# One written order from the end of attention on: expert 0 spread over five units, routing in thirds, seven-product outputs from the first chunk

## The chip, the cores and the metric

The kernel runs on one core of a Trainium2 chip. The core has five engines with a queue each: TensorE (PE in the profile, with its weight loads shown as PEld), VectorE (DVE), ScalarE (ACT), GpSimd (POOL) and SyncE (SP). The metric is the device time of one execution in microseconds; the median of three runs is quoted. Lower is better.

## The reference

Two parts follow each other. The first is attention over 4 batches, 8 heads, 768 tokens of 64 elements, in 8 blocks of 96 tokens; a small matrix per head, normalised five times, mixes the blocks of keys and values. The second is a mixture of 8 experts over all 3,072 tokens, and every expert works on every token:

```
x = attn_out.transpose(0, 2, 1, 3).reshape(3072, 512)
P = exp(x @ w_gate - max)
for _ in range(8):
    P /= P.sum(1, keepdims=True) + 1e-9
    P /= P.sum(0, keepdims=True) + 1e-9
    P *= N / E
for e in range(8):
    h = maximum(x @ w1[e], 0)          # 512 -> 1024
    out += P[:, e:e+1] * (h @ w2[e])   # 1024 -> 512
```

The eight rounds that normalise P need the logits of all tokens, so they can't start before attention has ended, and no expert's output can be weighted before they are done.

## The kernel before

**Attention and expert 0.** Attention goes batch by batch. While a batch of attention is computed, expert 0 is applied to the batch before it, by the plain formula, unweighted; its outputs are kept in `osbl` (24 tiles of 128 tokens) and are scaled by P later (`scale0`, two tiles at a time on ACT). So when attention ends, expert 0 is still to be done for the last batch: two runs of 384 tokens, each with eight hidden steps (four 384-column products and a relu, L299 and L301) and three output tiles of eight 512-column products in two halves (L306), with a copy (L314).

**Experts 1 to 7.** The tokens are cut into three chunks of 1,024 per expert, 21 chunks in all. The product of two 2 x 2 block matrices is formed with seven block products instead of eight. For the hidden layer, `hidden` does it for one of the four column groups of a chunk; this is called a unit. Its steps `p1` to `p7` are two 512-column products each (L508), with copies and relus on ACT and relu sums on DVE (L497) in between. It needs sums of weight blocks (`sum_w`, on GpSimd) and of token blocks (`sum_x`, three parts `p` of the tokens, four operations each on DVE, L454, one of which overwrites a part of the token matrix `xtT`). A unit with `fork` copies its first product into a second PSUM bank and accumulates on both; a unit without it keeps a copy in SBUF and adds it on DVE.

For the outputs, `Pair` does the same with two tiles of 128 tokens: steps `q1` to `q7`, four 256-column products each (L631). It needs sums of hidden blocks (`sums`, three operations on GpSimd, L621), a difference `s3` (`rest`), and sums of second-layer weights (`sum_w2`, eight operations on GpSimd, L444). `plain` is the ordinary form of an output tile: eight 512-column products (L597). Results are weighted by P and added to `osbl` on DVE (`gather`, L581).

**The order.** `pin` keeps an instruction in program order on its engine; what isn't pinned is placed by a scheduler, which moves instructions of one engine past one another. From the end of attention to L695 the work is in three generators: expert 0's last batch (`tail0`), the routing (`balance`, eight rounds of five DVE operations, a product with a matrix of ones that sums over the partitions, and three more DVE operations) and `sum_x`. They run beside the four units of the first chunk, which are without `fork` and, like the routing, not pinned:

```
works, n = [first_units(), tail0], 0
while works:
    works = [w for w in works if next(w, 0) is None]
    n += 1
    if n % 3 == 0:
        next(chain, 0)
        next(xs, 0)
```

Then comes the main loop over `r` (L722), all of it pinned. Turn `r` does unit `r % 4` of chunk `1 + r // 4`, step by step in turn with output steps: those of the first chunk in the plain form for `r` up to 4 (`flat`), and from `r = 5` on those of pair `r - 5` and the rest of the pair before it. `weights(n)` issues n operations of GpSimd's queue of weight sums. At its end the last two pairs of the last chunk are done in the plain form.

**PSUM.** Eight banks: five in a ring for hidden products, three in a ring (`oacc`) for outputs.

Of the kernel before, what the change touches and what calls it, by code (L numbers as in the profile page):

```python
# [25 lines left out]
def kernel(  # L26
# [394 lines left out]
    def ring(name, n):  # L421
        tiles = [ps.tile([128, 512], F32, name=f"{name}{j}") for j in range(n)]
        at = [0]

        def take():
            at[0] += 1
            return tiles[(at[0] - 1) % n]
        return take

# [6 lines left out]
    def sum_w2(e):  # L436
        w2s[e] = (wcp.tile([128, 4, 4, Dm // 2], BF16, name="w2e") if e % 2 else
                  w2q.tile([128, 4, 4, Dm // 2], BF16, name="w2s"))
        for k in (0, 2):
            b11, b12 = (w2t[e][:, k:k + 2, d:d + 256] for d in (0, 256))  # L440
            b21, b22 = (w2t[e][:, 4 + k:6 + k, d:d + 256] for d in (0, 256))
            t1, t2, t3, t4 = (w2s[e][:, j, k:k + 2, :] for j in range(4))
            for a, b, c in ((b12, b11, t1), (b22, t1, t2), (b22, b12, t3), (b21, t2, t4)):
                pin(nc.gpsimd.tensor_tensor(out=c, in0=a, in1=b, op=ALU.subtract))  # L444
                yield
# [3 lines left out]
    def sum_x(p):  # L449
        ta, tb = (slice(1024 * p + 512 * i, 1024 * p + 512 * i + 512) for i in range(2))  # L450
        b11, b12, b21, b22 = (xtT[:, k:k + 2, t] for k in (0, 2) for t in (ta, tb))
        x1, x2, x4 = (xc[:, j, :, 512 * p:512 * p + 512] for j in range(3))
        for a, b, c in ((b12, b11, x1), (b22, x1, x2), (b22, b12, b12), (b21, x2, x4)):
            pin(nc.vector.tensor_tensor(out=c, in0=a, in1=b, op=ALU.subtract))  # L454
            yield

    def balance(bank):
        onesc = mpc.tile([128, 128], F32)
        nc.vector.memset(onesc, 1.0)
        I128 = mpc.tile([128, 128], F32)  # L460
        nc.vector.tensor_copy(I128, Ibig)
        gm = mpc.tile([128, 1], F32)
        nc.vector.reduce_max(out=gm, in_=glog.rearrange("p t e -> p (t e)"), axis=AX.X)
        gmps = bank()[:, 0:128]
        nc.tensor.matmul(gmps[0:1, :], gm, I128, start=True, stop=True)
        gm1 = mpc.tile([1, 1], F32)
        nc.vector.reduce_max(out=gm1, in_=gmps[0:1, :], axis=AX.X, negate=True)
        yield
        gnps = bank()[:, 0:128]
        nc.tensor.matmul(gnps[:, 0:1], onesc[0:1, :], gm1, start=True, stop=True)  # L470
        gneg = mpc.tile([128, 1], F32)
        nc.vector.tensor_copy(gneg, gnps[:, 0:1])
        nc.scalar.activation(out=glog, in_=glog, func=AF.Exp, bias=gneg)

        rs2 = mpc.tile([128, NT], F32)
        cs2 = mpc.tile([128, E], F32)
        cs1 = mpc.tile([128, E], F32)
        yield
        for it in range(8):
            nc.vector.reduce_sum(out=rs2, in_=glog, axis=AX.X)  # L480
            nc.vector.tensor_scalar_add(rs2, rs2, 1e-9)
            nc.vector.reciprocal(out=rs2, in_=rs2)
            nc.vector.tensor_mul(glog, glog, mkap(rs2, [rs2.ap[0], rs2.ap[1], [0, E]]))
            nc.vector.reduce_sum(out=cs2, in_=glog.rearrange("p t e -> p e t"), axis=AX.X)  # L484
            csps = bank()[:, 0:128]
            nc.tensor.matmul(csps[:, 0:E], onesc, cs2, start=True, stop=True)
            nc.vector.tensor_scalar(out=cs1, in0=csps[:, 0:E], scalar1=float(E) / N,
                                    scalar2=1e-9 * E / N, op0=ALU.mult, op1=ALU.add)
            nc.vector.reciprocal(out=cs1, in_=cs1)
            nc.vector.tensor_mul(glog, glog, mkap(cs1, [cs1.ap[0], [0, NT], cs1.ap[1]]))  # L490
            yield
# [7 lines left out]
    def hidden(e, p, i, hT, s3, fork, hold, bank):  # L499
# [6 lines left out]
        def add(ps, wa, xa, first):  # L506
            for kk in range(2):
                hold(nc.tensor.matmul(ps, wa[:, kk, :], xa[:, kk, :],  # L508
                                      start=(first and kk == 0), stop=(kk == 1),
                                      skip_group_check=True))  # L510
# [14 lines left out]
        def p1():  # L525
            t["u"] = bank()
            add(t["u"], a11, b11, True)
            if fork:
                t["w"] = bank()
                hold(nc.scalar.copy(t["w"], t["u"]))  # L530
            else:
                t["p1"] = wide("p5")
                hold(nc.scalar.copy(t["p1"], t["u"]))

        def p2():
            if fork:
                add(t["w"], a12, b21, False)
                hold(relu(c11, t["w"]))
            else:
                w = bank()  # L540
                add(w, a12, b21, True)
                hold(relu_sum(c11, w, t["p1"]))

        def p6():
            add(t["u"], s2, x2, False)
            t["u2"] = wide("u2")
            hold(nc.scalar.copy(t["u2"], t["u"]))  # L547

        def p5():
# [3 lines left out]
            hold(nc.scalar.copy(t["p5"], t["v"]))  # L553

        def p7():
            add(t["u"], s3w, x3, False)
            hold(relu_sum(c22, t["u"], t["p5"]))

        def p3():
            add(t["v"], s4, b22, False)  # L560
            hold(relu_sum(c12, t["v"], t["u2"]))

        def p4():
            add(t["u"], a22, x4, False)
            hold(relu(c21, t["u"]))

        def rest():
            if s3 is None:
                pass
            elif fork:  # L570
                hold(nc.vector.scalar_tensor_tensor(out=s3[:, i, :], in0=t["w"], scalar=0.0,  # L571
                                                    in1=c12, op0=ALU.max, op1=ALU.subtract))
            else:
                hold(nc.vector.tensor_tensor(out=s3[:, i, :], in0=c11, in1=c12,
                                             op=ALU.subtract))

        return ([p1, p5, p6, p2, p7, p3, p4] if fork else [p1, p2, p6, p5, p7, p3, p4]), rest
# [92 lines left out]
    free = lambda ins: ins  # L670
    with banks("bk", 5) as bk, banks("op", 3) as op:
        bank = lambda: bk.tile([128, 512], F32, name="bk")
        tail0 = expert0(B - 1, lambda: hTb[1], bank,
                        lambda: op.tile([128, Dm], F32, name="oacc"))
        chain, xs = balance(bank), sum_x(0)
        for step in "TTCXTTTXCXXTTCTTTC":
            next({"T": tail0, "C": chain, "X": xs}[step])
        xs = sum_x(1)

        def first_units():  # L680
            for i in range(4):
                for f in hidden(1, 0, i, hTb[0], None, False, free, bank)[0]:
                    f()
                    yield

        works, n = [first_units(), tail0], 0
        while works:
            works = [w for w in works if next(w, 0) is None]
            n += 1
            if n % 3 == 0:  # L690
                next(chain, 0)
                next(xs, 0)
        for w in (chain, xs):
            for _ in w:
                pass  # L695

    ps = ctx.enter_context(banks("ps", 1))
    bank, obank = ring("bk", 5), ring("oacc", 3)
    xs = sum_x(2)
    queue = [sum_w2(1)]  # L700

# [9 lines left out]
    flat = [f for i in range(4) for j in range(2) for f in plain(1, 0, 4 * j + i, hTb[0], obank)]  # L711
    flat = [flat[0:8], flat[8:16], flat[16:24], flat[24:28], flat[28:32]]
    pairs = [Pair(e, p, i, hT, s3) for e, p, hT, s3 in chunks[1:] for i in range(4)]
# [7 lines left out]
    scale0([0, 4])  # L721
    for r in range(len(pairs) + 6):  # L722
        n, i = 1 + r // 4, r % 4
        if n < C:
            e, p, hT, s3 = chunks[n]
            if i == 0 and (n == 1 or p == 0) and e + 1 < E:
                load_w1(e + 1)
                queue.append(sum_w(e + 1))
            if r == 4 or p == 1 and i == 2 and n > 1 and e + 1 < E:
                load_w2(2 if r == 4 else e + 1)  # L730
                queue.append(sum_w2(2 if r == 4 else e + 1))
            steps, rest = hidden(e, p, i, hT, s3, r > 1, pin, bank)
        else:
            steps, spares, rest = spares[:7], spares[7:], None
        k = r - 5
        if k + 1 in range(len(pairs)):
            pairs[k + 1].sums()
        weights(4 if r < 4 else 1 + i % 2)
        now = pairs[k] if k in range(len(pairs)) else None
        if r < 5:  # L740
            outs = flat[r]
        else:
            outs = [f for a, b in ((now, "q5"), (before, "q7"), (now, "q1"), (before, "q4"),
                                   (now, "q6"), (now, "q2"), (now, "q3")) if a
                    for f in [getattr(a, b)]]
        for j in range(max(len(steps), len(outs))):
            if j < len(steps):
                steps[j]()
                if j == 3 and n < C:
                    if r < 12 and r != 3:  # L750
                        q = r + 1 if r < 3 else r
                        scale0([8 * (q // 4) + q % 4, 8 * (q // 4) + q % 4 + 4])
                    if k + 1 in range(len(pairs)):
                        pairs[k + 1].keep()
            if j < len(outs):
                outs[j]()
            if j == 1 and late:
# [37 lines left out]
```

## Time and profile before

| | us |
|---|---|
| median of 3 runs (685.52 to 685.59) | 685.56 |
| profiled execution | 686.2 |
| its span | 684.4 |
| PE busy in the span | 658.6 (96%) |
| DVE busy | 473.4 (69%) |
| ACT busy | 375.4 (55%) |
| GpSimd busy | 444.3 (65%) |

The profile shows one execution. Times in it count from the span's start. A row of a timeline gives the start, the length, the engine, the line of the kernel, the operation, what it writes and reads, and how often it stands there in a row; where the engine was idle before, the time and what ended it follow in brackets. Records of products overlap, so the distance of two starts says more on PE than a length. The granted clock of PE was 0.997 of full speed over the span.

### The profile page before, as it was taken

To read this page: it belongs to the slowest core of one execution; us is meant where nothing else is said; L and a number is where in the kernel's file an instruction comes from. 1 tells how busy PE (TensorE), PEld (TensorE's weight loads), DVE (VectorE), ACT (ScalarE), POOL (GpSimd) and SP (SyncE) were. 2 spreads that over 40 slices of the span, in tenths; PEclk is the share of its full clock that TensorE was granted. 3 is DMA by queue.
4 is the path that set the end of the run, shared out by engine and by line. 5 is a ranking of instruction groups with operands and counts; after the bars stand their busy time and mean duration, and the time that the engine had idled before them with its cause. 6 is when DMAs were issued, how large, how long until landed. Compare 5 with 4: busy or idle time off the path is not lost.

```text
span 684.4 us, 13128 instructions
## 1 busy us (share of the span) xinstructions
PE 658.6 (96%) x5011; PEld 428.7 (63%) x5088; DVE 473.4 (69%) x977; ACT 375.4 (55%) x725; POOL 444.3 (65%) x417
## 2 busy tenths in 40 slices
PE   5989999999999999999999999999999999999996
PEld 2646666644446666666666666666666666666665
DVE  6627555578656777777777777777777777777775
ACT  3746646345667765555555555555555555555540
POOL 4542324201929888959797887879796979846640
PEclk9999999999999999999999999999999999999998
DMA  9898833403040304030303021030403040000223
GB/s 147 167 215 127 142 75 63 63 0 62 0 63 1 62 1 62 2 62 1 62 2 57 6 39 24 4 61 1 63 1 61 1 62 1 2 1 36 88 100 148
DMA packets 31904, 36.57 MB, mean 53 GB/s; under 512 B 2016, under 2 KB 24288, under 8 KB 31840
## 3 DMA queue, kind: packets, MB, share of 16 engines
q0 software_dynamic: 26400, 27.82, 25.4%
q1 hardware_dynamic: 5440, 7.90, 3.4%
q8 instruction: 40, 0.66, 0.4%
q14 instruction: 24, 0.20, 0.1%
HBM read 52.45 MB, written 6.29 MB: 86 GB/s over the span
## 4 chain that ended last, share of the span: by engine, by line
PE 87%; DVE 5%; DMA 4%; issue 2%; ACT 1%; POOL 1%; SPq 0%; DVEq 0%; ACTq 0%; POOLq 0%
PE oacc L631 35%; PE bk L508 34%; PE bank L306 4%; PE bank L299 4%; DMA qt<-in_q_dram 3%; PE oacc L597 2%; PE bank L232 1%; PE bk L597 1%; DVE hT L497 1%; DMA vsb<-vs 1%; PE bank L215 1%; PE bank L196 1%; PE bank L243 1%; DVE cs L484 0%; PE bk L299 0%
## 5 line engine op out<-in xcount | busy, mean ns | idle before, releaser
L581 DVE SCALAR_TENSOR_TENSOR osbl<-oacc,glog,osbl 128x256 f32<-128x256 f32 (+1 forms) x398 | 214.6, 540 | 131.8 <-PE oacc L631 114.0
L494 ACT ACTIVATE hT<-bk 128x512 bf16<-128x512 f32 x162 | 96.7, 597 | 143.1 <-PE bk L508 133.2
L508 PE MATMUL bk<-xtT,w1e 128*128 128x512 bf16 x478 | 144.3, 379 | 1.9 <-ACT hT L494 0.7
L631 PEld LDWEIGHTS <-hs 128*128 128x128 bf16 x936 | 91.6, 98 | 59.8 <-issue 0.3
L621 POOL TENSOR_TENSOR hs<-hT 128x512 bf16<-128x512 bf16 x78 | 90.5, 1160 | 48.8 <-DVE hT L497 43.3
L631 PEld LDWEIGHTS <-hT 128*128 128x128 bf16 x860 | 84.1, 98 | 55.9 <-issue 1.5
L631 PE MATMUL oacc<-w2e,hT 128*128 128x256 bf16 x752 | 112.8, 273 | 1.4 <-DVE osbl L581 1.0
L631 PE MATMUL oacc<-w2e,hs 128*128 128x256 bf16 x648 | 97.2, 273 | 0.6
L508 PE MATMUL bk<-xc,wc 128*128 128x512 bf16 x319 | 96.3, 379 | 0.0
L621 POOL TENSOR_TENSOR hs<-hT,hs 128x512 bf16<-128x512 bf16 x78 | 90.0, 1154 | 6.1
L621 POOL TENSOR_TENSOR hs<-hs,hT 128x512 bf16<-128x512 bf16 x78 | 90.0, 1154 | 6.1
L508 PEld LDWEIGHTS <-w1e 128*128 128x128 bf16 x672 | 65.8, 98 | 18.4 <-issue 4.6
L497 DVE CUSTOM_DVE_ANT_0 hT<-bk,p 128x512 bf16<-128x512 f32 x90 | 62.2, 691 | 10.2 <-PE bk L508 3.0
L553 ACT COPY p<-bk 128x512 f32<-128x512 f32 x84 | 49.2, 585 | 26.6 <-PE bk L508 23.9
L547 ACT COPY u<-bk 128x512 f32<-128x512 f32 x84 | 49.2, 586 | 24.8 <-PE bk L508 22.3
L497 DVE CUSTOM_DVE_ANT_0 hT<-bk,u 128x512 bf16<-128x512 f32 x84 | 57.1, 680 | 0.0
L508 PEld LDWEIGHTS <-wc 128*128 128x128 bf16 x504 | 49.3, 98 | 10.8 <-issue 0.2
L530 ACT COPY bk<-bk 128x512 f32<-128x512 f32 x78 | 44.5, 571 | 19.9 <-PE bk L508 19.9
L571 DVE SCALAR_TENSOR_TENSOR s<-bk,hT 128x512 bf16<-128x512 f32 x78 | 53.1, 681 | 0.0
L508 PE MATMUL bk<-xc,w1e 128*128 128x512 bf16 x159 | 48.0, 379 | 1.7 <-DVE hT L497 1.6
L508 PE MATMUL bk<-xtT,wc 128*128 128x512 bf16 x159 | 48.0, 379 | 0.5
L444 POOL TENSOR_TENSOR w2e<-w2e 128x512 bf16<-128x512 bf16 x32 | 36.8, 1162 | 15.9 <-PE oacc L306 6.8
(120 smaller groups left out, 869.7 us busy)
## 6 DMA issues: line engine op xcount, KB each, us to landing
w1e<-in_moe_w_dram POOLq DMA_DIRECT2D x8, 1024.0 KB, 8.0
w2e<-in_moe_w_dram POOLq DMA_DIRECT2D x8, 1024.0 KB, 8.8
out_dram<-osbl SPq DMA_DIRECT2D x23, 256.0 KB, 2.0
vt<-in_v_dram POOLq DMA_DIRECT2D x3, 768.0 KB, 10.9
vsb<-vs SPq DMA_DIRECT2D x16, 97.5 KB, 5.1
vsb<-vs POOLq DMA_DIRECT2D x16, 97.5 KB, 4.7
qt<-in_q_dram POOLq DMA_DIRECT2D x4, 384.0 KB, 12.9
kt<-in_k_dram POOLq DMA_DIRECT2D x4, 384.0 KB, 13.5
```

The source lines that it names most:

```text
L299: hold(nc.tensor.matmul(hps[:, 0:n], w1t[e][:, kk, fb * 128:(fb + 1) * 128], xtT[:, kk, c0:c0 + n], start=(kk == 0), stop=(kk == 3)))
L444: pin(nc.gpsimd.tensor_tensor(out=c, in0=a, in1=b, op=ALU.subtract))
L494: relu = lambda o, x: nc.scalar.activation(out=o, in_=x, func=AF.Relu)
L497: return nc.vector._custom_dve(TENSOR_ADD_SAT, out=o, in0=x, in1=y, s0=TOP, s1=0.0)
L508: hold(nc.tensor.matmul(ps, wa[:, kk, :], xa[:, kk, :], start=(first and kk == 0), stop=(kk == 1), skip_group_check=True))
L530: hold(nc.scalar.copy(t["w"], t["u"]))
L547: hold(nc.scalar.copy(t["u2"], t["u"]))
L553: hold(nc.scalar.copy(t["p5"], t["v"]))
L571: hold(nc.vector.scalar_tensor_tensor(out=s3[:, i, :], in0=t["w"], scalar=0.0, in1=c12, op0=ALU.max, op1=ALU.subtract))
L581: pin(nc.vector.scalar_tensor_tensor(out=o, in0=ps, scalar=glog[:, t, e:e + 1], in1=o, op0=ALU.mult, op1=ALU.add))
L621: pin(nc.gpsimd.tensor_tensor(out=s[:, c], in0=a, in1=b, op=o))
L631: pin(nc.tensor.matmul(ps, h[:, fb, :], w[:, fb, :], start=(first and fb == 0), stop=(fb == 3), skip_group_check=True))
```

## The change

From the end of attention on there is one written order on every engine; everything is pinned.

- Expert 0's last batch is a generator `last_dense`. Thirteen of its 28 steps run first, in turn with the first seven parts of the routing and the first `sum_x`; the other fifteen are put into the first five turns of the main loop, three in each, as their output steps.
- A round of the routing is three parts (row sums and their reciprocal; row scaling and column sums; the sum over partitions, its reciprocal and column scaling). The 26 parts of the routing end with turn 4.
- The main loop starts at the first chunk (`n = r // 4`), whose four units are now with `fork` (their `s3` is formed on GpSimd), and has four turns more. Pairs are formed for the first chunk too; `flat` is gone.
- The second `sum_x` is on GpSimd, the first and third stay on DVE. The sums of second-layer weights change buffers between odd and even experts.
- The routing's products use the ring of three banks, which expert 0's steps use as well; two of expert 0's output tiles use banks of the ring of five.

```diff
-    def sum_x(p):
+    def sum_x(p, eng):
...
-            pin(nc.vector.tensor_tensor(out=c, in0=a, in1=b, op=ALU.subtract))
+            pin(eng.tensor_tensor(out=c, in0=a, in1=b, op=ALU.subtract))
...
         for it in range(8):
-            nc.vector.reduce_sum(out=rs2, in_=glog, axis=AX.X)
...
-            csps = bank()[:, 0:128]
+            pin(nc.vector.reduce_sum(out=rs2, in_=glog, axis=AX.X))
+            pin(nc.vector.tensor_scalar_add(rs2, rs2, 1e-9))
+            pin(nc.vector.reciprocal(out=rs2, in_=rs2))
+            yield
+            pin(nc.vector.tensor_mul(glog, glog, mkap(rs2, [rs2.ap[0], rs2.ap[1], [0, E]])))
+            pin(nc.vector.reduce_sum(out=cs2, in_=glog.rearrange("p t e -> p e t"), axis=AX.X))
+            yield
+            csps = obank()[:, 0:128]
+            pin(nc.tensor.matmul(csps[:, 0:E], onesc, cs2, start=True, stop=True))
...
         def rest():
-            if s3 is None:
-                pass
...
+            if first:
+                pin(nc.gpsimd.tensor_tensor(out=s3[:, i, :], in0=c11, in1=c12,
+                                            op=ALU.subtract))
             else:
...
-        return ([p1, p5, p6, p2, p7, p3, p4] if fork else [p1, p2, p6, p5, p7, p3, p4]), rest
+        return [p1, p5, p6, p2, p7, p3, p4], rest
...
+    def last_dense():
+
+        for c in range(2):
+            c0 = (B - 1) * S + c * 384
+            if c == 0:
+                h = [hTb[1][:, fb, 0:384] for fb in range(8)]
+            else:
+                two = [hsp.tile([128, 4, 384], BF16, name="hs") for _ in range(2)]
+                h = [two[fb // 4][:, fb % 4, :] for fb in range(8)]
+            for fb in range(8):
+                hps = obank()[:, 0:384]
+                for kk in range(4):
+                    pin(nc.tensor.matmul(hps, w1t[0][:, kk, fb * 128:(fb + 1) * 128],
+                                         xtT[:, kk, c0:c0 + 384],
+                                         start=(kk == 0), stop=(kk == 3)))
+                pin(relu(h[fb], hps))
+                yield
+            for tt in range(3):
+                oacc = rings["bk"][(1, 4)[tt]] if c == 0 and tt < 2 else obank()
+                for fb in range(8):
+                    pin(nc.tensor.matmul(oacc, h[fb][:, tt * 128:(tt + 1) * 128],
+                                         w2t[0][:, fb, :], start=(fb == 0), stop=(fb == 7)))
+                    if fb == 3:
+                        yield
+                pin(nc.scalar.copy(osbl[:, c0 // 128 + tt, :], oacc))
+                yield
+
+    dense, chain, xs = last_dense(), balance(), sum_x(0, nc.vector)
+    for step in "TTCXTTXCXXTTCCTTTCCTTCTT":
+        next({"T": dense, "C": chain, "X": xs}[step])
+
+    queue = [sum_x(1, nc.gpsimd), sum_w2(1)]
...
-    pairs = [Pair(e, p, i, hT, s3) for e, p, hT, s3 in chunks[1:] for i in range(4)]
+    pairs = [Pair(e, p, i, hT, s3) for e, p, hT, s3 in chunks for i in range(4)]
...
-    scale0([0, 4])
+    weights(2)
     for r in range(len(pairs) + 6):
-        n, i = 1 + r // 4, r % 4
+        n, i = r // 4, r % 4
...
-        weights(4 if r < 4 else 1 + i % 2)
+        weights((2, 4, 4, 2, 0)[r] if r < 5 else 4 if r < 8 else 1 + i % 2)
...
         if r < 5:
-            outs = flat[r]
+            outs = [None, lambda: next(dense), None, lambda: next(dense), None,
+                    lambda: next(dense)]
...
+        if r == 5:
+            for _ in chain:
+                pass
+            scale0([0, 4])
...
-            if j < len(outs):
+            if j < len(outs) and outs[j]:
                 outs[j]()
+            if r < 5 and j in (0, 1, 3, 4, 5):
+                if (5 * r + (0, 1, 0, 2, 3, 4)[j]) % 4 != 3:
+                    next(chain, 0)
```

## The prediction

> **What bounds the kernel now.** The page's busy shares come first: PE 96%. The chain of waits, by line, puts 35% on L631 (output products) and 34% on L508 (hidden products), so the end is set by PE's stream of products and by the holes in it. The timeline of PE says what a product costs and where the stream is full:
>
> ```profile
> 182.59 0.59 PE L508 MATMUL bk<-xtT,w1e 128*128 128x512 bf16 x2
> 183.02 0.59 PE L597 MATMUL oacc<-w2e,hT 128*128 128x512 bf16 x2
> ...
> 211.66 0.59 PE L508 MATMUL bk<-xtT,w1e 128*128 128x512 bf16 x2
> ...
> 217.73 0.59 PE L508 MATMUL bk<-xtT,w1e 128*128 128x512 bf16 x2
> ...
> 223.81 0.59 PE L508 MATMUL bk<-xtT,w1e 128*128 128x512 bf16 x2
> ```
>
> Two 512-column products start 0.432 us before the next two, so one takes 0.216 us (its record lasts longer because records overlap), and 256 columns take half. From 211.66 on every unit (14 hidden products, 28 half-wide output products) takes 6.08 us, and 28 x 0.216 is 6.05: nothing is left there. The stretch ahead of it is looser, as the table by stretches shows (length, then busy time of PE, PEld, DVE, ACT, POOL):
>
> ```profile
> 133.83:175.26 41.43, 37.70 (x187) 17.61 (x189) 32.27 (x90) 20.80 (x40) 7.30 (x7) 1.00 0.15 26
> 175.26:205.73 30.47, 29.08 (x131) 13.11 (x134) 18.30 (x28) 18.79 (x32) 18.18 (x17) 1.00 0.24 35
> 205.73:211.66 5.93, 5.64 (x35) 3.30 (x35) 2.86 (x6) 4.43 (x8) 5.77 (x6) 1.00 0.00 0
> ```
>
> At 133.83 expert 0's last batch starts; at 175.26 the loop's unit 0; at 205.73 unit 5, the first with the seven-product outputs; 211.66 is unit 6. The first stretch holds 49,152 columns of expert 0 and 28,672 of the first four units: 152 products' worth, 32.8 of 41.4 us. What interrupts them is the routing chain, one round of which reads on DVE and PE:
>
> ```profile
> 142.44 0.35 DVE L480 TENSOR_REDUCE rs<-glog 128x24 f32<-128x192 f32 x1
> ...
> 143.77 0.50 DVE L484 TENSOR_REDUCE cs<-glog 128x8 f32<-128x192 f32 x1
> 144.32 0.39 PE L486 MATMUL bk<-cs,onesc 128*128 128x8 f32 x2 [0.25 <-DVE cs L484]
> 144.57 1.02 PE L508 MATMUL bk<-xtT,w1e 128*128 128x512 bf16 x4
> ...
> 145.19 0.36 DVE L490 TENSOR_TENSOR glog<-glog,cs 128x192 f32<-128x192 f32 x1
> 145.58 0.35 DVE L480 TENSOR_REDUCE rs<-glog 128x24 f32<-128x192 f32 x1
> ```
>
> A round is 3.14 us from start to start, 2.66 of it on DVE, and its column sum takes PE 0.25 us (144.32 to 144.57).
>
> **The change, part by part.** Everything ahead of 133.83 stays in its order on every engine, and the last units (spares, last pairs, stores) have the same form, with four more units of the loop ahead of them. So I compare 133.83 to unit 6, which is 77.83 us now, with the same path in the new order plus four steady units, which the new loop has more of.
>
> *Products.* Expert 0's 49,152 columns and five hidden units of 14 products: 96 + 70 = 166, by 0.216 = 35.9 us. The plain outputs of the first chunk (32,768 columns) become four pairs (28,672), counted in the four extra units: 4 x 6.08 = 24.3 us. That alone is 4,096 columns, 1.7 us, less.
>
> *Column sums.* Two set-up products and eight sums, now at fixed places: 10 x 0.25 = 2.5 us, as now.
>
> *The first column sum.* PE reaches it after nine steps of expert 0, near 140.5 (133.83 + 8 x 0.65 + 0.87 and two set-up products). On DVE the four x sums of the first third of tokens stand ahead of it, 0.69 us each now; undisturbed, cs is done at nearly the same time (1.82 us from a round's first row to cs, begun near 138.7): a wait of 0.1. New is that GpSimd computes x sums (the second third) at the same time. Rows of this meeting:
>
> ```profile
> 180.25 1.16 POOL L332 TENSOR_TENSOR w1e<-w1e 128x512 bf16<-128x512 bf16 x1
> 181.36 1.61 POOL L332 TENSOR_TENSOR wc<-w1e,wc 128x512 bf16<-128x512 bf16 x1
> 180.81 1.14 DVE L454 TENSOR_TENSOR xc<-xtT 128x1024 bf16<-128x1024 bf16 x1
> 187.29 0.87 DVE L454 TENSOR_TENSOR xc<-xtT,xc 128x1024 bf16<-128x1024 bf16 x1
> 170.90 0.35 DVE L490 TENSOR_TENSOR glog<-glog,cs 128x192 f32<-128x192 f32 x1
> ```
>
> A DVE x sum beside a GpSimd one took 1.14 or 0.87 instead of 0.69. Bounds for the four: 0 and 1.8 us; I take 0.32 each, the mean of both stretched rows, as GpSimd has four double-length sums queued just then: 1.3. With the 0.1 the wait is 1.4 us. The routing product at 170.90 ran beside a GpSimd sum too (L444, 168.55 to 177.9) and kept its 0.35, so I leave the rounds unstretched.
>
> The Trainium skill (GPSIMD Engine Reference, Key points) says GpSimd shares its SBUF interfaces with VectorE and contends with its instructions that have two SBUF inputs. By that rule the two products of a round (0.36 us each) stretch as the x sums did, by 1.14/0.69: 0.47 us a round. The x-sum rows agree, the 170.90 row does not. The sum by the rule: x sums all at 1.14, 0.5 us more, and the rounds at 4.6 us, still under the 4.7 of the next part, so some 681.1.
>
> *Rounds against units.* Seven further rounds lie over the rest of expert 0 and the five units. A round needs 3.14 us, and the ten relu sums (0.69 each) that stand between its parts on DVE add 1.0: 4.1 us. PE offers a round every 4.7 us (33 us over seven). So the sums are ready, with 0.6 us to spare each. But a relu sum behind a third is late for the fourth product of its unit, which waits for it: today's such waits are 0.40 and 0.66 us (PE at 173.98 and 199.81). Bounds: 0 and 5 x 0.66 = 3.3; laid out in order only one unit collides, by 0.2, so I stay near the lower end: 0.5.
>
> *Ring of five banks.* With one product fewer per unit at the front (no output step stands between a unit's first and second hidden product), the second product of a unit needs the bank that the previous unit's last relu reads. Product, relu, next product on a freed bank:
>
> ```profile
> 173.98 0.59 PE L508 MATMUL bk<-xc,w1e 128*128 128x512 bf16 x2 [0.40 <-DVE hT L497]
> 174.61 0.60 ACT L494 ACTIVATE hT<-bk 128x512 bf16<-128x512 f32 x1 [1.67 <-PE bk L508]
> 175.26 0.59 PE L508 MATMUL bk<-xtT,w1e 128*128 128x512 bf16 x2 [0.69 <-ACT hT L494]
> ```
>
> That is 1.28 us from that product to the reuse; two pairs of products cover 0.87. So 0.41 us in units 1, 2 and 3, and 0.16 in unit 4, where a column sum lies between: 1.4 us. Bounds 0 and 4 x 0.41.
>
> *ACT and DVE.* The first four units take the form of the later ones: ACT copies the first product into a second bank and does that relu itself, so DVE has one relu sum (0.69) less per unit and ACT one relu (0.60) more. A unit's five ACT passes (0.57, 0.59, 0.59, 0.60, 0.60) plus three for expert 0 (0.49 or 0.59) are 4.4 of some 5.2 us: hidden, but first in, first out.
>
> *Unit 5.* The two scalings of output tiles (1.33 us for two, row 175.10 on ACT) now come right behind the last round and ahead of the copy that this unit's third product needs. Counted from the last column sum: relu to 1.49, scalings to 2.82, copy to 3.43; unit 5 starts at 0.68 and would want the copy at 2.42: 1.0 us, then 0.55 for the copy of the output part behind it. Its seven pairs of hidden products and five output groups are 12 x 0.433 = 5.2 us, so 6.8 in all. Unit 5 takes 5.93 now, 0.7 of it waits; bounds 5.9 and 6.8; I take 6.8, since the order is fixed.
>
> *GpSimd.* Added: four 1,024-column sums (about 2.3 us each, twice the 1.16 of 512) and four first-unit differences (1.16). The eight second-weight sums (9.3 us) write another buffer and no longer wait 6.8 us for expert 0's outputs (L444's releaser, PE oacc L306). From 134 GpSimd has until about 169, when pair 0's sums start: 9.2 + 9.3 + 4.6 us fit. The load of expert 2's first weights leaves from the same queue behind the third difference, near 164, and takes 8.0 us; its sums are reached near 177. Nothing on the path; what it costs if late is a rival. SP's queue (stores alone) isn't passed by anything.
>
> *Sum.* 35.9 + 2.5 + 1.4 + 0.5 + 1.4 + 6.8 + 24.3 = 72.8 against 77.8: 5.0 us less. The profiled execution (686.2, span 684.4) becomes 681.2; it stands 0.6 above the median, which becomes 680.6.
>
> **The rivals.**
> - *Only the columns remain.* Expert 0's steps rotate through three banks that the column sums use too, each freed by an in-order engine. If its fifteen steps inside the units each wait 0.2 us (the small waits of the first stretch today), 3.0 us come back: 683.6. For it: ACT at 85% in these units. Against: each step's bank was filled two steps earlier.
> - *GpSimd late.* Pair 2's sums stand behind four weight sums. If the load takes over 18 us instead of 8.0, the outputs of unit 7 wait; 3.5 us for a set of sums, 684.1. Against: 5 us to spare.
> - *The rounds set the pace: slower.* The place is DVE's queue in units 0 to 4. PE now waits in program order at every column sum, with all products behind it, where the old order let them be rearranged around it. From 4.7 us a round, each 0.1 us costs 0.7 us; above 5.4 us a round the gain is gone; at 5.7 it costs 7 us, 687.6. For it: DVE is about 83% busy there (28 of 34 us). Against: it needs 1.3 us more in each round than the rows give, and no row of the rounds is stretched.
>
> **How the numbers follow.** The forecast has 0.70, only-the-columns 0.12 (0.08 faster, 0.04 same), GpSimd late 0.04 (0.01 faster, 0.03 same), the pace of the rounds 0.14. Hence faster 0.79, same 0.07, slower 0.14, with 0.2% (1.4 us, about what a measurement here can tell) as the border. The range: no stretched x sum, no collision and unit 5 as now give 680.6 - 1.3 - 0.5 - 0.9 = 677.9; stretched x sums at 1.14 and every unit colliding give 680.6 + 0.5 + 2.8 = 683.9. With the two small-gain rivals inside: 677.8 to 684.3.
>
> **What would show it.** Right: unit 6's first product near 182.3 (133.83 + 48.5), then 6.08 us a unit; one wait of one to two us ahead of the first column sum and hardly any at the seven others; waits of 0.2 to 0.4 us on a relu at the second product of units 1 to 4; about 1 us on ACT's copy in unit 5; x sums on DVE over 0.8 us. Wrong: waits of PE on cs in most rounds, holes at expert 0's steps in the units, or unit 6 after 187.3, from where on nothing is gained (211.66 - 24.3).

## The result and the profile after

The changed kernel takes 689.96 us (median of 4 runs, 689.26 to 690.61) against 685.58 for the kernel before on the same chip: 4.4 us more, a ratio of 1.0063 (95% interval 1.0045 to 1.008). The prediction said 680.6 us, and faster with a chance of 0.79. It was wrong, sign included.

The table by stretches of the changed kernel answers the one shown of before (length, then busy time of PE, PEld, DVE, ACT, POOL with their counts; then the granted clock of PE, the DMA share and GB/s). The stretches are: expert 0's first product to unit 0, units 0 to 4, unit 5, and from unit 6 to the end.

```profile
134.60:154.74 20.14, 12.80 (x60) 5.90 (x59) 16.12 (x23) 5.21 (x11) 14.65 (x8) 0.92 0.00 1
154.74:184.61 29.87, 28.40 (x146) 14.24 (x144) 24.96 (x58) 18.85 (x36) 14.21 (x13) 1.00 0.20 36
184.61:191.67 7.06, 5.69 (x35) 3.31 (x34) 4.94 (x10) 5.88 (x11) 6.82 (x7) 1.00 0.00 0
191.67:688.10 496.43, 491.57 (x3409) 333.29 (x3407) 363.66 (x652) 274.31 (x512) 388.92 (x344) 1.00 0.19 37
```

Cut at the same places, the prediction's sum reads: columns for 44 products and three small ones ahead of unit 0, 10.3 us, and the wait of 1.4, so 11.7; then 6.8 for unit 5; and 30.0 for units 0 to 4 as the rest of 48.5. Units 0 to 4 came out within 0.2 us, unit 5 within 0.3. Nearly the whole miss lies in the first stretch: 20.14 us instead of 11.7, so 8.4 of the 8.7 us by which the profiled execution (689.85) is over its forecast (681.2). The rest nearly cancels: the stretch starts 0.8 us later than in the kernel before, and from unit 6 on it is 0.6 us less. In the first stretch PE was busy 12.8 of the 20.14 us, at a mean granted clock of 0.92, the only one of the four below 1.00. The list of PE's waits in this stretch and in the units behind it (in total, how many, longest):

```profile
PE oacc L492 <- DVE cs L489: 4.4, 1, 4.4
PE oacc L470 <- DVE gm L468: 1.5, 1, 1.5
PE oacc L676 <- DVE gneg L477: 1.4, 1, 1.4
...
PE oacc L625 <- DVE osbl L575: 1.3, 1, 1.3
PE bk L514 <- ACT hT L500: 0.8, 3, 0.3
PE oacc L492 <- DVE cs L489: 0.5, 1, 0.5
```

The first three are the first stretch: PE waits 7.3 us for DVE, where the prediction had 1.4 in a single place. The last three are units 0 to 5, 2.6 us together. So the question is why DVE is late between 134 and 149. The timeline of GpSimd and of DVE there:

```profile
134.91 2.11 POOL L459 TENSOR_TENSOR xc<-xtT 128x1024 bf16<-128x1024 bf16 x1 [10.10 <-issue]
137.10 2.12 POOL L459 TENSOR_TENSOR xc<-xtT,xc 128x1024 bf16<-128x1024 bf16 x1
139.18 2.56 POOL L459 TENSOR_TENSOR xtT<-xtT 128x1024 bf16<-128x1024 bf16 x1
141.71 2.56 POOL L459 TENSOR_TENSOR xc<-xtT,xc 128x1024 bf16<-128x1024 bf16 x1
144.24 1.59 POOL L449 TENSOR_TENSOR w2s<-w2e 128x512 bf16<-128x512 bf16 x1
145.91 1.48 POOL L449 TENSOR_TENSOR w2s<-w2e,w2s 128x512 bf16<-128x512 bf16 x1
147.35 1.14 POOL L449 TENSOR_TENSOR w2s<-w2e 128x512 bf16<-128x512 bf16 x1
...
135.55 1.56 DVE L466 CAST I<-Ibig 128x128 f32<-128x128 bf16 x1
137.03 0.34 DVE L468 TENSOR_REDUCE gm<-glog 128x1 f32<-128x192 f32 x1
138.14 1.63 DVE L459 TENSOR_TENSOR xc<-xtT 128x1024 bf16<-128x1024 bf16 x1
139.80 2.49 DVE L459 TENSOR_TENSOR xc<-xtT,xc 128x1024 bf16<-128x1024 bf16 x1
142.22 0.14 DVE L477 COPY gneg<-oacc 128x1 f32<-128x1 f32 x1
142.29 2.54 DVE L459 TENSOR_TENSOR xtT<-xtT 128x1024 bf16<-128x1024 bf16 x1
144.74 1.63 DVE L459 TENSOR_TENSOR xc<-xtT,xc 128x1024 bf16<-128x1024 bf16 x1
146.67 0.75 DVE L485 TENSOR_SCALAR rs<-rs 128x24 f32<-128x24 f32 x1
147.79 0.92 DVE L488 TENSOR_TENSOR glog<-glog,rs 128x192 f32<-128x192 f32 x1
148.74 0.49 DVE L489 TENSOR_REDUCE cs<-glog 128x8 f32<-128x192 f32 x1
```

Compare ends. GpSimd's second x sum ends at 139.22 (137.10 + 2.12), the third at 141.74, the fourth at 144.27, the first weight sum at 145.83. DVE's four x sums end at 139.77, 142.29, 144.83 and 146.37: each 0.54 to 0.56 us after a GpSimd instruction's end. The cast of the identity, 0.16 us in the kernel before, ends 0.09 us after GpSimd's first x sum; the `TENSOR_SCALAR` of 24 elements, 0.18 before, ends 0.03 us after a weight sum. So a DVE instruction isn't slowed in proportion: it stands still until the GpSimd instruction that is running has ended, and is done after that within its own time (0.69, 0.16 and 0.18 us alone), less some 0.1 us. In turn GpSimd's next instruction has its time plus 0.45 (2.56 instead of 2.11, 1.59 instead of 1.14). The reductions (L468 0.34, L489 0.49) and the copy from PSUM (L477, 0.14) kept the lengths that they have elsewhere, in the middle of it all.

The Trainium skill (SBUF — State Buffer, Who interferes with whom) says just this: a DVE instruction with two SBUF inputs, or a cast or `tensor_scalar` in a two-port mode, and a GpSimd instruction that reads SBUF exclude one another for the whole instruction, whichever starts first, while reductions are never held. These rows agree point by point, though they don't show in which mode a cast or a `TENSOR_SCALAR` ran.

What follows from it on PE's queue, where every product stands behind these waits in program order:

```profile
142.42 1.67 PE L676 MATMUL oacc<-xtT,w1e 128*128 128x384 bf16 x8 [1.40 <-DVE gneg L477]
...
149.38 0.36 PE L492 MATMUL oacc<-cs,onesc 128*128 128x8 f32 x2 [4.43 <-DVE cs L489]
149.60 4.44 PE L684 MATMUL bk<-w2e,hT 128*128 128x512 bf16 x12
153.87 1.03 PE L684 MATMUL oacc<-w2e,hT 128*128 128x512 bf16 x4
```

Twelve products from 149.60 to 153.87 are 0.356 us each, not 0.216: 1.7 us more. The granted clock was 0.50 from 149.96 to 153.38 and 1.00 on both sides of it. The account of the first stretch: 10.3 us of work, 7.8 of waits, 1.7 of low clock, 0.3 of small holes. The waits are 7.3 in the list, which counts from the end of a record; as records of products overlap, the three holes from start to start are 1.6, 1.6 and 4.6 us.

### The profile page after: what moved, and what is told of

It is laid out like the page before. It is cut to its first block, busy times and chain, and to the rows that moved or that the text cites. A ratio compares the mean times of both kernels' runs of the same rounds, so it can differ in the third digit from the quotient of the medians.

```text
span 688.1 us, 13352 instructions
## 1 busy us (share of the span) xinstructions
PE 662.0 (96%) x5136; PEld 434.6 (63%) x5136; DVE 485.3 (71%) x979; ACT 379.5 (55%) x736; POOL 473.5 (69%) x437
## 3 DMA queue, kind: packets, MB, share of 16 engines
HBM read 52.45 MB, written 6.29 MB: 85 GB/s over the span
## 4 chain that ended last, share of the span: by engine, by line
PE 89%; DMA 4%; DVE 4%; POOL 1%; issue 1%; ACT 0%; SPq 0%; POOLq 0%; DVEq 0%; ACTq 0%
PE oacc L625 36%; PE bk L514 36%; PE bank L306 4%; PE bank L299 4%; DMA qt<-in_q_dram 4%; PE bank L232 1%; PE bk L591 1%; PE oacc L684 1%; DVE xc L459 1%; DMA vsb<-vs 1%; PE bank L215 1%; PE bank L196 1%; PE bk L684 1%; PE bank L243 1%; PE unread L344 1%
## 5 line engine op out<-in xcount | busy, mean ns | idle before, releaser
L575 DVE SCALAR_TENSOR_TENSOR osbl<-oacc,glog,osbl 128x256 f32<-128x256 f32 (+1 forms) x410 | 219.0, 535 | 125.8 <-PE oacc L625 117.7
L514 PE MATMUL bk<-xtT,w1e 128*128 128x512 bf16 x504 | 149.9, 379 | 0.0
L625 PEld LDWEIGHTS <-hs 128*128 128x128 bf16 x984 | 96.2, 98 | 63.2 <-POOL hs L615 0.5
L625 PEld LDWEIGHTS <-hT 128*128 128x128 bf16 x904 | 88.4, 98 | 59.8 <-issue 2.6
L615 POOL TENSOR_TENSOR hs<-hT 128x512 bf16<-128x512 bf16 x82 | 95.2, 1161 | 36.6 <-DVE hT L503 31.1
L615 POOL TENSOR_TENSOR hs<-hT,hs 128x512 bf16<-128x512 bf16 x82 | 95.3, 1162 | 6.4
L615 POOL TENSOR_TENSOR hs<-hs,hT 128x512 bf16<-128x512 bf16 x82 | 94.8, 1156 | 6.4
L625 PE MATMUL oacc<-w2e,hs 128*128 128x256 bf16 x616 | 92.4, 273 | 0.0
L503 DVE CUSTOM_DVE_ANT_0 hT<-bk,p 128x512 bf16<-128x512 f32 x84 | 58.0, 691 | 6.5 <-PE bk L514 1.5
L625 PE MATMUL oacc<-w2s,hs 128*128 128x256 bf16 x368 | 55.2, 273 | 0.0
## 6 DMA issues: line engine op xcount, KB each, us to landing
vt<-in_v_dram POOLq DMA_DIRECT2D x3, 768.0 KB, 10.3
```

The lines of the kernel that those rows point to most:

```text
L503: return nc.vector._custom_dve(TENSOR_ADD_SAT, out=o, in0=x, in1=y, s0=TOP, s1=0.0)
L514: pin(nc.tensor.matmul(ps, wa[:, kk, :], xa[:, kk, :], start=(first and kk == 0), stop=(kk == 1), skip_group_check=True))
L575: pin(nc.vector.scalar_tensor_tensor(out=o, in0=ps, scalar=glog[:, t, e:e + 1], in1=o, op0=ALU.mult, op1=ALU.add))
L615: pin(nc.gpsimd.tensor_tensor(out=s[:, c], in0=a, in1=b, op=o))
L625: pin(nc.tensor.matmul(ps, h[:, fb, :], w[:, fb, :], start=(first and fb == 0), stop=(fb == 3), skip_group_check=True))
```

## The experiments

All medians are beside the kernel before on the same chip (685.8 to 686.0 us). None of the kernels leaves work out. Lines of the code are those of the changed kernel, unless another kernel is named.

**1. GpSimd's x sums held back.** A copy on GpSimd that reads the first column sum's input keeps its x sums behind it.

```diff
...
+        if n == 13:
+            pin(nc.gpsimd.tensor_copy(held2, seen["cs2"][:, 0:2]))
```

> One small GpSimd copy is added that reads the first round's column sums, so that GpSimd's first x sum can't start before them; nothing else is changed. Theory A (a DVE instruction with two SBUF inputs, or a copy within SBUF, waits for the GpSimd sum that is running): DVE's four x sums are 0.69 us again instead of 1.6 to 2.5 and the cast 0.16 instead of 1.56; from expert 0's first product to unit 0 it is 11 to 12 us instead of 20.1; the whole 681 to 683 us. Theory B (the written order itself makes PE wait: the column sum stands too early): the wait of some 4 us on cs stays, 689 to 690 us.

Measured: 684.7 us (684.29 to 686.75, 10 runs), ratio 0.9984 (0.9973 to 0.9995). The table by stretches (first two rows), then DVE and PE in the first two rounds:

```profile
133.93:144.53 10.60, 10.50 (x59) 5.51 (x58) 8.86 (x20) 5.54 (x11) 3.62 (x3) 1.00 0.01 2
144.53:179.38 34.85, 30.20 (x142) 14.55 (x144) 29.82 (x62) 19.16 (x36) 23.96 (x20) 0.95 0.19 31
...
138.25 0.69 DVE L459 TENSOR_TENSOR xc<-xtT,xc 128x1024 bf16<-128x1024 bf16 x1
...
141.70 1.62 DVE L500 TENSOR_TENSOR glog<-glog,cs 128x192 f32<-128x192 f32 x1
143.74 1.59 DVE L489 TENSOR_SCALAR rs<-rs 128x24 f32<-128x24 f32 x1
145.70 1.88 DVE L492 TENSOR_TENSOR glog<-glog,rs 128x192 f32<-128x192 f32 x1
...
148.24 0.39 PE L496 MATMUL oacc<-cs,onesc 128*128 128x8 f32 x2 [3.11 <-DVE cs L493]
```

The same instructions in the same order, but without GpSimd beside them: the first stretch takes 10.60 us instead of 20.14, and DVE's x sums are back at 0.69. So the order as such costs nothing there. The total missed what I expected of the theory (681 to 683), because the hold only moved: GpSimd's x sums now meet the end of round 0 and round 1, whose products and `TENSOR_SCALAR` take 1.6 to 1.9 us instead of 0.36 and 0.18. PE waits 3.11 us at the next column sum, its clock falls again (0.50 from 148.81 to 152.22), and the units take 34.85 us.

**2. GpSimd's x sums cut into quarters,** at their old place.

```diff
+        parts = 4 if eng is nc.gpsimd else 1
...
+            for j in range(parts):
+                w = 512 // parts
+                cut = slice(w * j, w * j + w)
+                pin(eng.tensor_tensor(out=c[:, :, cut], in0=a[:, :, cut], in1=b[:, :, cut],
+                                      op=ALU.subtract))
```

> Each of GpSimd's four x sums is cut into four of a quarter of the columns; same work, same order. Theory A, by whole instructions (DVE waits until the running GpSimd instruction ends): DVE's x sums wait for at most some 0.6 us each, 1.3 us instead of 1.6 to 2.5, and the stretch ahead of unit 0 is 15 to 17 us instead of 20.1; the whole 685 to 687 us. Theory C (both share a port by turns of elements): the stretch and the time stay, 689 to 691 us. Theory B: also unchanged.

Measured: 682.24 us (681.91 to 682.48, 4 runs), ratio 0.9943 (0.9928 to 0.9959). GpSimd has the same bytes to sum, in instructions of 0.66 us, up to 1.14 where DVE is in their way; two of its groups of four and three of DVE's x sums beside them:

```profile
137.37 3.89 POOL L463 TENSOR_TENSOR xc<-xtT,xc 128x256 bf16<-128x256 bf16 x4
141.23 2.77 POOL L463 TENSOR_TENSOR xtT<-xtT 128x256 bf16<-128x256 bf16 x4
...
136.92 1.04 DVE L463 TENSOR_TENSOR xc<-xtT,xc 128x1024 bf16<-128x1024 bf16 x1
137.95 1.08 DVE L463 TENSOR_TENSOR xtT<-xtT 128x1024 bf16<-128x1024 bf16 x1
138.96 1.15 DVE L463 TENSOR_TENSOR xc<-xtT,xc 128x1024 bf16<-128x1024 bf16 x1
```

A shorter instruction holds DVE for less: the first stretch takes 11.76 us, PE's waits on column sums 1.6 in all, the granted clock stays at 1.00. Nothing was moved and no work was saved; the 7.7 us between the two medians come from the length of GpSimd's instructions alone. It is also better than I expected of theory A (15 to 17 us, 685 to 687), in part by luck: the cast (135.01) and the first x sum (136.20) started on the border between two GpSimd instructions, of which one ended at 135.03 and one at 136.31, and kept their 0.16 and 0.69 us.

**3. The second third's x sums back on DVE,** in the units; GpSimd starts with its weight sums (1.16 us each).

```diff
-    queue = [sum_x(1, nc.gpsimd), sum_w2(1)]
+    queue = [sum_w2(1)]
+    xs = sum_x(1, nc.vector)
```

> The second third's x sums go back to DVE, one at the end of each of units 0 to 3; GpSimd begins with the second-layer weight sums (1.16 us each), which wait for nothing. Theory A: the weight sums hold DVE as well, by up to 1.2 us each: x sums of 1.1 to 1.9 us, the stretch ahead of unit 0 14 to 16 us, the units a little longer for DVE's added sums; the whole 685 to 688 us. If only the x sums on GpSimd are to blame: 11 to 12 us ahead of unit 0, 682 to 683 us. Theory B: 689 to 690 us.

Measured: 685.85 us (683.57 to 687.65, 10 runs), ratio 0.9998 (0.9985 to 1.001). DVE's x sums take 1.66, 1.53, 1.57 and 1.64 us beside weight sums of 1.16 to 1.60; the first stretch takes 16.39 us (14 to 16 expected) with a wait of 2.9 on the first column sum, the units 29.80. With experiment 2 and the changed kernel this gives the hold by length: a DVE x sum of 0.69 takes 1.04 to 1.15 us beside GpSimd instructions that take 0.66 alone, 1.5 to 1.7 beside 1.15, and 2.5 beside 2.11. Where it is held in full, that is the GpSimd instruction's own length plus some 0.45 us. That the four extra x sums on DVE left the units at 29.80 also says that DVE's queue had room for them.

**4. The clock.** Seventeen products that nobody reads fill most of the longest wait.

```diff
+        if n == 16:
+            for _ in range(17):
+                pin(nc.tensor.matmul(rings["bk"][0], Ibig,
+                                     mkap(Ibig, [Ibig.ap[0], [0, 4], [1, 128]]),
+                                     start=True, stop=True))
```

> Leaves nothing out; adds 17 products of 512 columns whose sums nobody reads, on TensorE right ahead of the first column sum, where it waits 4.43 us in the changed kernel. 17 x 0.216 = 3.7 us, so they end before cs does (149.38) and no instruction of another engine moves. Theory A1 (part of the loss is that TensorE's clock falls behind the long wait: 12 products took 0.356 us each instead of 0.216, 1.7 us): the wait at the column sum shrinks to 0.7 us, the twelve products take 0.22 us each, unit 0 starts near 153.0 instead of 154.74, and the total is near 688.3. Theory A2 (the products behind the wait are slow because of their data or their banks): the wait shrinks as well, but the twelve still take 0.36 us each, unit 0 starts at 154.7 and the total stays at 690.

Measured: 689.3 us (688.12 to 689.71, 4 runs), ratio 1.0045 (1.0031 to 1.0059). PE's timeline:

```profile
144.99 3.83 PE L696 MATMUL bk<-Ibig 128*128 128x512 bf16 x17
149.59 0.36 PE L492 MATMUL oacc<-cs,onesc 128*128 128x8 f32 x2 [0.77 <-DVE cs L489]
149.81 2.75 PE L684 MATMUL bk<-w2e,hT 128*128 128x512 bf16 x12
...
216.44 0.61 PE L625 MATMUL oacc<-w2s,hs 128*128 128x256 bf16 x4 [1.32 <-POOL hs L615]
```

The column sum runs at the same time as in the changed kernel (149.59; 149.38 there), so nothing else moved, and the same twelve products now take 2.59 us to the next row (149.81 to 152.40) instead of 4.27. The stretch to unit 0 is 18.46 us, 1.68 less, with the granted clock at 1.00: the low clock behind the wait is what made them slow, and theory A1 holds. The Trainium skill (TensorE: Matmul & The Clock Gate, Part 1) says that the clock is halved after an idle window of about 3.4 us and comes back after as long a busy one; a wait of 4.43 us and a low clock of 3.41 us agree. Two shorter waits, 3.11 us in experiment 1 and 2.91 in experiment 3, had the same low clock behind them, so here less idle time than the 3.4 us was enough. The total is 1.0 us over the 688.3 that I expected, and the profiled execution gained little (span 687.9 against 688.1): 1.3 us go again at 216.44, in a wait for GpSimd's hidden sums, which stand behind a weight sum whose load took 10.2 us here (203.88 to 214.12) and 8.9 in the changed kernel (205.34 to 214.25). That is the rival "GpSimd late", at another load than the one I named, and at a third of the price.

**5. One part of the change alone.** In the kernel before, only the second third's x sums go to GpSimd.

```diff
...
-        xs = sum_x(1)
+        xs = sum_x(1, nc.gpsimd)
```

> One part of the change alone, in the kernel before, whose scheduler places the routing: its x sums of the second third go from VectorE to GpSimd and nothing else moves. Theory A (VectorE's instructions with both operands in SBUF are held until the running GpSimd instruction ends, whatever the order): the four VectorE x sums take 1.0 to 2.5 us instead of 0.69, row sums' tensor_scalar and the routing products stretch beside GpSimd's 2.1 to 2.5 us sums, the first column sum comes 3 to 5 us later, TensorE waits for it (the old order has more products to put ahead, so less than 4.4), and the total is 687 to 691, slower by 1 to 5 us, though four sums (2.8 us) leave VectorE's queue. Theory B (it is the fixed order that makes the held instructions cost time; the old order puts products ahead of them): no wait over 1 us on a column sum, and 684 to 686, no change or a little faster.

Measured: 691.79 us (690.88 to 692.6, 4 runs), ratio 1.0083 (1.0067 to 1.0098): 5.8 us slower, a little more than I expected of theory A. Here is DVE's second x sum, PE at the first column sum (it waited 0.27 us there in the kernel before, at 141.18), and the stretch behind it:

```profile
139.50 2.49 DVE L454 TENSOR_TENSOR xc<-xtT,xc 128x1024 bf16<-128x1024 bf16 x1
...
146.92 0.60 PE L486 MATMUL bk<-cs,onesc 128*128 128x8 f32 x2 [3.16 <-DVE cs L484]
...
146.90:150.50 3.60, 3.58 (x11) 1.76 (x12) 2.42 (x8) 0.49 (x1) 0.00 (x0) 0.50 0.00 0
```

The old order has the same collision, waits in the same places (1.36 on the maximum, 3.16 on cs) and the same fall of the clock, to 0.50, for twice as long (145.50 to 152.32). So it isn't the fixed order that made the held instructions cost time: these four instructions on the other engine cost more than the whole change lost. One part of my expectation failed: the rounds did not stretch, since in this order no weight sums follow on GpSimd until 175.

**6. Experiments 1 and 2 together.**

> The changed kernel with both earlier edits: GpSimd's x sums of the second third begin only after the first column sum, and are cut in quarters of 256 columns a row. Theory A (the hold lasts as long as the running GpSimd instruction): the stretch to unit 0 is 10.6 us as with the first edit, and round 1 is held by 0.4 us an instruction instead of 1.2, so that the units take 30.3 instead of 34.85; unit 5 7.06; total near 680.4. Rival C (the hold depends on how much work GpSimd has in all, not on the length of an instruction): the units stay near 34 us and the total near 684.

Measured: 680.25 us (679.98 to 680.99, 4 runs), ratio 0.9917 (0.9904 to 0.9931). The table by stretches:

```profile
145.09:175.09 30.00, 28.39 (x146) 14.26 (x145) 25.03 (x58) 18.84 (x36) 25.78 (x28) 1.00 0.21 36
175.09:182.15 7.06, 5.69 (x36) 3.31 (x35) 4.94 (x10) 5.88 (x11) 6.82 (x7) 1.00 0.00 0
182.15:678.50 496.35, 491.51 (x3409) 333.28 (x3407) 363.85 (x652) 274.38 (x512) 388.83 (x344) 1.00 0.19 37
```

From expert 0's first product (134.49) to unit 0 it is 10.60 us. Unit 6 starts at 182.15, where the prediction had 182.3 for the change itself. GpSimd has as much to sum as in the changed kernel, so rival C falls: it is the length of an instruction and its place, not the amount.

**7. All x sums on DVE, GpSimd held back, its weight sums halved,** and two edits of unit 5 (below).

```diff
-                pin(nc.gpsimd.tensor_tensor(out=c, in0=a, in1=b, op=ALU.subtract))
+                for k1 in ((0, 1) if e == 1 else (slice(0, 2),)):
+                    pin(nc.gpsimd.tensor_tensor(out=c[:, k1], in0=a[:, k1], in1=b[:, k1],
+                                                op=ALU.subtract))
...
-    queue = [sum_x(1, nc.gpsimd), sum_w2(1)]
+    queue = [sum_w2(1)]
+    xs = sum_x(1, nc.vector)
...
-        if r == 4:
+        if r == 5:
             xs = sum_x(2, nc.vector)
...
-            scale0([0, 4])
+            scale0([4])
...
+            if r == 5 and j == 1:
+                scale0([0])
+            if r == 7 and j == 2:
+                next(xs, 0)
```

> The changed kernel without a GpSimd sum beside a round or an x sum that TensorE waits for: the second third's x sums go back to VectorE, one a unit; GpSimd starts its second-weight sums after the first column sum and has them in halves (128x256); the last third's x sums start one unit later, and the second scaling of unit 5 goes behind the copy that its third product needs. Theory A: 10.6 to 11 us to unit 0, units 29.8 to 30.5, unit 5 6.2 to 6.6 instead of 7.06, total 679 to 680.5, which is where the prediction for the change itself lay. If the collision were not the cause, it stays above 685. If the sums back on VectorE make the rounds set the pace, as one rival of the prediction had it, the units take 32 us or more, with waits on cs in several of them.

Measured: 680.8 us (680.62 to 681.09, 5 runs), ratio 0.9924 (0.9912 to 0.9937). 10.60 us to unit 0, units 30.21, unit 5 6.29, all as expected of theory A. The total is 0.3 us over the range expected: 497.30 us from unit 6 on instead of 496.4. Waits of 0.25 (a relu behind the x sums that moved) and 0.24 (GpSimd's hidden sums) are in the list; the rest is not. The rounds didn't set the pace with four more x sums in DVE's queue.

**8 to 10. What unit 5 waits for.** The kernel of experiment 6, with one or both of the edits of unit 5: the scaling of output tile 0 goes behind ScalarE's copies (8); the last third's x sums move one unit later (9); both (10).

```diff
-        if r == 4:
+        if r == 5:
             xs = sum_x(2, nc.vector)
...
-            scale0([0, 4])
+            scale0([4])
...
+            if r == 5 and j == 1:
+                scale0([0])
...
-            if j == 5:
+            if j == (2 if r == 8 else 5):
                 next(xs, 0)
```

> The kernel with GpSimd's x sums held back and quartered, and in unit 5 only the scaling of output tile 4 stays ahead; that of tile 0 goes behind ScalarE's two copies. It tells apart what the second output group of unit 5 waits for (1.35 us). Theory S (the prediction's own term: two scalings, 1.33 us, ahead of the copies): the wait falls by 0.6 us and unit 5 takes 6.45 instead of 7.06. Theory X (VectorE's x sum, 1.64 us instead of 0.69 because it meets GpSimd's hidden sums, ends last, and the gather stands behind it): unit 5 stays at 7.0 to 7.1.

> As the one before, but the scalings stay and the x sums of the last third move one unit later (units 5 to 8 instead of 4 to 7), so that none stands ahead of unit 5's first gather. Theory S: unit 5 stays at 7.06. Theory X: the gather waits for the scalings alone, which end 0.2 us before the x sum does now: unit 5 takes 6.8, the prediction's figure, and nothing is lost behind it.

> Both edits of unit 5. Scaling of tile 4 and the gather are then free of each other's queue: unit 5 takes 6.3 us, as in the variant with all x sums on VectorE, and units from 6 on stay at 496.4 in sum: 0.75 us under the kernel with the two GpSimd edits, near 679.5. If an x sum in unit 8 holds that unit's last product back, up to 0.7 us come back: 680.2.

The second group of outputs of unit 5 waits for the first gather on DVE. In the kernel of experiment 6 that gather (177.37) has two things ahead of it, a scaling on ACT and an x sum on DVE; below them, the group's wait there and in experiment 10:

```profile
175.92 1.33 ACT L670 ACTIVATE osbl<-osbl,glog 128x512 f32<-128x512 f32 x2
...
175.81 1.64 DVE L463 TENSOR_TENSOR xc<-xtT 128x1024 bf16<-128x1024 bf16 x1
177.37 0.47 DVE L584 SCALAR_TENSOR_TENSOR osbl<-oacc,glog,osbl 128x256 f32<-128x256 f32 x1
...
177.90 0.60 PE L634 MATMUL oacc<-w2e,hT 128*128 128x256 bf16 x4 [1.35 <-DVE osbl L584]
```

```profile
176.74 0.60 PE L634 MATMUL oacc<-w2e,hT 128*128 128x256 bf16 x4 [0.66 <-DVE osbl L584]
```

Experiments 8 and 9 have one run each, 680.11 and 680.51 us. Unit 5 takes 6.96 us (8), 6.99 (9) and 6.28 (10). The scalings end at 177.25 and the x sum at 177.45, so with one out of the way the other is just as late: experiment 8 bears out theory X, experiment 9 theory S, and my 6.8 for the latter was a miss. Only both together free the gather. Experiment 10 takes 679.83 us (679.28 to 680.5, 5 runs), ratio 0.9909 (0.9894 to 0.9923), the lowest median of all, some 6 us under the kernel before. Its interval overlaps that of experiment 6, so the total alone doesn't show it to be the faster of the two; from unit 6 on it has 497.0 us instead of 496.4, which takes most of unit 5's gain back.

## Why the prediction was wrong

- **The first column sum: the step that failed.** The term was 1.4 us; the waits on the maximum, on its negative and on cs are 7.3 by the list, and the low clock behind the last adds 1.7. The meeting of the two engines was seen, and even its place; it was priced by the wrong rule. I took a stretch per x sum (0.32 us, from rows beside GpSimd sums of 1.16 us), where the hold lasts until the running GpSimd instruction ends, and the ones queued there take 2.1 to 2.6 us; I had called them double-length in the same paragraph. Both rows that I averaged follow that rule already: the x sum at 180.81 ends at 181.95, 0.54 us after GpSimd's row from 180.25 (181.41), and the one at 187.29 ends at 188.16, 0.55 us after a GpSimd sum that runs from 186.46 for 1.15 us (187.61). What I read as a factor was the rest of a GpSimd instruction that was still running. The bound of 1.8 us was no bound for the same reason. The cast in front, which decides when the maximum is known, and the `TENSOR_SCALAR` weren't counted at all.
- **"The routing product at 170.90 ... kept its 0.35, so I leave the rounds unstretched."** One row was read as evidence against the rule that I cited from the Trainium skill (GPSIMD Engine Reference, Key points). Two of GpSimd's eight sums there, in the kernel before:

```profile
169.78 1.16 POOL L444 TENSOR_TENSOR w2e<-w2e 128x512 bf16<-128x512 bf16 x1
170.90 1.36 POOL L444 TENSOR_TENSOR w2e<-w2e 128x512 bf16<-128x512 bf16 x1
```

One ends at 170.94 and the next starts at 170.90, so DVE's row began on the border between two instructions. This time GpSimd was the one held: its sum took 1.36 us instead of 1.15. The row is no evidence against the rule; the measurement sides with the Trainium skill. My sum by that rule (681.1) was as wrong, because it again scaled durations instead of adding holds.
- **Rounds against units, ring of five banks.** 0.5 and 1.4 us forecast. The ring came out as said: at the second product of units 1, 2 and 3 the list has 0.25 each, and from start to start the holes are 0.41 to 0.42 (such as 160.20 to 161.04, less the 0.432 of two products). The one wait on a column sum is 0.55 in the list and 0.7 from start to start. The routing products and the `TENSOR_SCALAR` were held there too (1.15 and 1.04, and 0.63, in the round from 160.58), so the cover that I counted on was thinner than thought, and it was enough: 29.87 us against 30.0. The rival "the rounds set the pace" had the right sign and the wrong place: what decided was one wait in front of the units, not a rate within them.
- **Unit 5.** 6.8 forecast, 7.06 measured. The scalings were half of the reason; an x sum on DVE, itself held to 1.64 us, ends 0.2 us after them.
- **Products, column sums, four extra units.** Right for the products and the extra units. A column sum costs 0.14 to 0.16 us where PE doesn't wait for it (155.17 to 155.31), not the 0.25 that I took from rows with a wait, some 0.6 us less over the units, which made up for the longer wait there. Experiment 6 is the change without that collision and comes to 680.25 us, which is near the forecast of 680.6 by some luck: its first stretch lacks the stretched x sums that the forecast had, and its unit 5 is longer; steady units take 6.08 us (191.67, 197.75 and 203.82 in the changed kernel).
- **GpSimd: "nothing on the path".** True of its own queue in the changed kernel, where PE waits for none of its results. But the margin of 5 us that I gave is that of another load: with the load of the second-layer weights 1.3 us longer, experiment 4 lost 1.3 us to it. And an engine off the path held one that is on it.

## What to carry to other kernels

Work moved to GpSimd isn't free for DVE. As these runs have it: list which DVE instructions on the path will run beside it, and add to each up to the full length of the GpSimd instruction that may be running, not a share of its own length. If the two must overlap, cut GpSimd's work into short instructions, or start it behind the DVE work that PE waits for; both together turned a loss of 4.4 us into a gain of 5.7. And before a single row is held against a rule, look at what the other engine was doing at that very start.

## What was not expected of the hardware

- Tiny instructions are held as long as large ones: 24 elements a partition took 1.59 us instead of 0.18 (experiment 1), a 128-element cast 1.56 instead of 0.16.
- One wait of 4.43 us on PE costs about 6.1: the 1.7 us of low clock behind it come on top. The low clock came in one length: 0.50 for 3.41 us here, behind the 3.11 us of experiment 1 and behind the 2.91 of experiment 3 (145.42 to 148.84), and for 6.82 us, twice that, around the 3.16 of experiment 5; behind the two waits of 1.4 us in the changed kernel it stayed at 1.00 (137.0 to 149.3).
- Expert 0's first product starts between 133.93 and 134.80 in kernels whose code ahead of it is the same; in the changed kernel 0.7 us of that is a wait for a load of weights, at 41.10. A difference of that size between two profiles is no sign of what an edit did.
